# Attention and a gated feed-forward block: pair 0's transposes, the order of copies and loads on GpSimd, and the last output half

## The chip, the cores and the metric

The kernel runs on one core of a Trainium2 chip. The core has a matrix engine (TensorE, "PE" in the profile, whose weight loads are listed as "PEld"), VectorE ("DVE"), ScalarE ("ACT"), GpSimd ("POOL") and SyncE ("SP"). Each engine runs its own list of instructions in order and waits on semaphores that other engines and DMAs count up. DMAs are issued by SP, ACT and POOL and moved by 16 shared DMA engines. The metric is the device time of one execution in microseconds (us).

## The reference

The first part is softmax attention over 8 batches, 12 heads, 448 positions and 64 columns a head; the second is a feed-forward block on the 3584 x 768 result with weights of 768 x 1536 (gate and value) and 1536 x 768 (output). All inputs and the output are fp32.

```python
scores = scale * np.matmul(q, k.transpose(0, 1, 3, 2))
attn = softmax(scores)                       # over the last axis
x = np.matmul(attn, v).transpose(0, 2, 1, 3).reshape(B * S, H * D)
g = x @ w_gate
out = (g * (1.0 / (1.0 + np.exp(-g))) * (x @ w_val)) @ w_out
```

## The kernel before

**Tiling.** Heads are worked in pairs, 48 of them. The 448 positions of a head are 4 chunks of 112. For a pair, `qk_half` computes scores for two of the four chunks at a time, transposed (keys on the partitions): four matmuls of 448 columns into two double-bank PSUM tiles `s`, and one exponential on ScalarE for each tile (L194). `sums` adds up the exponentials with a matrix of ones, `recips` inverts the sums on VectorE, `pv` multiplies with V and `scaled` writes the normalized result into `X`, which is the transposed input of the feed-forward block. That block is cut into 8 pieces of 384 or 512 tokens. For each, `ffn1_steps` makes 12 gate and 12 value products with their activation, and `ffn2_steps` the output in chunks of 128 tokens, each in two halves of `OH` = 384 columns (12 accumulating matmuls per half, L252 or L255), copied from PSUM by ScalarE (L314) and stored.

**Operands of the scores.** Q and K must be turned so that the 64 head columns lie on the partitions. Three ways are used:
- Pair 0 is loaded as fp32 by SP, cast to fp16 by VectorE and ScalarE in `prep` (L153, L154; head 0 by the one, head 1 by the other), and turned by TensorE's transposes in `turn` (L170): eight for Q into one PSUM tile `tp`, a copy by VectorE (L172), a dummy matmul, eight for K into another tile, and a second copy (L176). Q lies in the upper half of `qkT` (columns from `NC` on), K in the lower.
- Pairs 1 to 10 are loaded as fp16 by POOL and turned by TensorE, 16 transposes and one copy each.
- Pairs from 11 (`NPE`) on are loaded by POOL, two pairs to a load (`load_qk16`: one DMA for Q, one for K, L118), copied by POOL into another order (`prep`, L156, two copies a pair), and turned by a DMA transpose issued by SP (L159).

**Order of the work.** It is written out by hand: every engine executes in the order in which the program issues. The loop over pairs `pr` issues for pair `pr` the first score half, the preparation of later pairs (`prep(pr + 3)` by POOL and SP, `prep(pr + 2)` where TensorE turns), pieces of the feed-forward block, and the second score half. At even `pr` from 8 on it first issues the load of pairs `pr + 6` and `pr + 7` on POOL's queue (L426 and L427), and then the two copies of `prep(pr + 3)` on the same queue (L438 and L439). V's loads (`load_v`, L127) and the weights' loads (L142, L144) use POOL's queue as well; the third part of `wo`, the output weights, is issued just ahead of the first of those even `pr`. A DMA of POOL waits for the landing of the DMA issued eight before it. `wo` is read for the first time by the output matmuls after piece 0 (L297 onwards), in thirds of four matmuls.

`dummy(n)` issues n matmuls of 512 columns on zeros. PSUM tiles come from three rings: `ps_s` (two tiles of two banks, for the scores), `ps_a` (one bank) and `ps_f` (three banks, for all else).

**The end.** The last 128 tokens' two halves have `osb` tiles of their own. The first half is copied by ScalarE and stored; the second half is one PSUM tile, copied as 192 columns by ScalarE (L309) and 192 by VectorE (L312), and then stored by two DMAs, 112 rows by SP and 16 rows by ACT (L324).

Of the kernel before, what the change touches and what calls it, by code (L numbers as in the profile page):

```python
# [10 lines left out]
FP32 = mybir.dt.float32  # L11
FP16 = mybir.dt.float16
AF = mybir.ActivationFunctionType
# [3 lines left out]
HS = 4096.0  # L17
# [3 lines left out]
LA = 6  # L21
# [6 lines left out]
def kernel(  # L28
# [23 lines left out]
    OH = DM // 2  # L52
# [41 lines left out]
    raw = {}  # L94
    v16 = {}
    qkT = {}
# [4 lines left out]
    def dummy(n):  # L101
        wp = ps_f.tile([128, 512], FP32, tag="f", name="wp")
        for _ in range(n):
            nc.tensor.matmul(wp[:], lhsT=warm[:, 0:128], rhs=warm[:], start=True, stop=True)
# [41 lines left out]
    def prep(pr):  # L146
        rq, rk = raw[pr]
        if pr == 0 or pr >= NPE:
            qk16 = attp.tile([P, 2, NC, 2, D], FP16, tag="qk16", bufs=3)
            for t, src in enumerate((rq, rk)):  # L150
                dst = qk16[:, 1 - t].rearrange("p c h d -> p h c d")
                if pr == 0:
                    nc.vector.tensor_copy(dst[:, 0], src[:, 0])  # L153
                    nc.scalar.activation(dst[:, 1], src[:, 1], AF.Copy)  # L154
                else:
                    nc.gpsimd.tensor_copy(dst, src)  # L156
        qkT[pr] = attp.tile([128, 2 * NC, P], FP16, tag="qkT", name="qkT", bufs=5)
        if pr >= NPE:
            nc.sync.dma_start_transpose(  # L159
                qkT[pr][:], qk16[:].rearrange("p t c h d -> p (t c h d)")  # L160
            )
            return None

        def turn():
            tp = ps_f.tile([128, 2 * NC, 128], FP16, tag="f", name="tp")
            for t in range(2):
                for c in range(NC):
                    for hx in range(2):
                        src = qk16[:, 1 - t, c, hx] if pr == 0 else raw[pr][t][:, hx, c, :]
                        nc.tensor.transpose(tp[ts(hx, 64), (1 - t) * NC + c, 0:P], src, ident[:])  # L170
                if pr == 0 and t == 0:
                    nc.vector.tensor_copy(qkT[pr][:, NC:], tp[:, NC:, 0:P])  # L172
                    dummy(1)
                    tp = ps_f.tile([128, 2 * NC, 128], FP16, tag="f", name="tp")
            hi = NC if pr == 0 else 2 * NC
            nc.vector.tensor_copy(qkT[pr][:, 0:hi], tp[:, 0:hi, 0:P])  # L176

        return turn

    def qk_half(pr, half, between=None):  # L180
        if half == 0:
# [68 lines left out]
    def mm(dst, lhsT, rhs, start, stop):  # L250
        if not tiled[0]:
            nc.tensor.matmul(dst, lhsT=lhsT, rhs=rhs, start=start, stop=stop)  # L252
            return
        for j in range(4):
            nc.tensor.matmul(  # L255
                dst[ts(j, 32), :], lhsT=lhsT[:, ts(j, 32)], rhs=rhs, start=start, stop=stop
            )
# [32 lines left out]

    def ffn2_steps(kk, c0, n, hts, last_block):
        for ch in range(n // 128):
            osb = fp.tile([128, DM], FP32, tag="osb", bufs=3)
            for oh in range(2):
                if last_block and ch == n // 128 - 1 and oh == 1:
                    osb = fp.tile([128, DM], FP32, tag="osb", bufs=3)
                op = ps_f.tile([128, 512], FP32, tag="f")  # L297
                for fb in range(NFB):
                    mm(
                        op[:, 0:OH],  # L300
                        lhsT=hts[:, fb, ts(ch, 128)],
                        rhs=wo[fb // (NFB // 3)][:, fb % (NFB // 3), ts(oh, OH)],
                        start=(fb == 0),
                        stop=(fb == NFB - 1),
                    )
                last = last_block and ch == n // 128 - 1
                if last and oh == 1:
                    m = OH // 2
                    nc.scalar.activation(  # L309
                        osb[:, OH : OH + m], op[:, 0:m], AF.Copy, scale=1.0 / HS  # L310
                    )
                    nc.vector.tensor_scalar_mul(osb[:, OH + m : DM], op[:, m:OH], 1.0 / HS)  # L312
                else:
                    nc.scalar.activation(osb[:, ts(oh, OH)], op[:, 0:OH], AF.Copy, scale=1.0 / HS)  # L314
                if oh == 1 or last:
                    m0, m1 = (oh * OH, oh * OH + OH) if last else (0, DM)
                    l0 = c0 + ch * 128
                    l = l0
                    while l < l0 + 128:
                        b, j = divmod(l, S)  # L320
                        c, p0 = divmod(j, P)
                        m = min(P - p0, l0 + 128 - l)
                        eng = nc.scalar if last and m < 64 else nc.sync
                        eng.dma_start(  # L324
                            out[ts(NB * kk + b, S), :].rearrange("(p c) m -> c p m", c=NC)[
                                c, p0 : p0 + m, m0:m1
                            ],
                            osb[l - l0 : l - l0 + m, m0:m1],
                        )
                        l += m  # L330
                yield NFB * OH / 2400.0
# [7 lines left out]
    with tc.manual_schedule():  # L339
# [82 lines left out]
        for pr in range(END):  # L422
            slots = 2 * (min([x for x in add_at if x > pr] + [END + 0.5]) - pr)
            odd = pr % 2 == 1
            turn2 = None
            if not odd and 14 <= pr + LA < NPAIR:  # L426
                load_qk16(pr + LA)  # L427
            if pr == FIRST:
                recip_act(pr - 2, sums(pr - 2))
                load_table("exp_and_others")  # L430
                halves = [pv(pr - 2, 0), pv(pr - 2, 1, ps_f)]
            if pr < NPAIR:
                qk_half(pr, 0, prep(2) if pr == 1 else None)
            if pr == 0:
                dummy(1)
                turn()
                dummy(1)
            if pr + 3 < NPAIR and pr + 3 >= NPE:  # L438
                prep(pr + 3)  # L439
            if pr + 2 < NPAIR:  # L440
                if 0 < pr < NPE - 2:
                    turn2 = prep(pr + 2)
                if (pr + 2) % GP == GP - 1 and 4 <= (pr + 2) // GP + 1 < NGRP:
                    load_v((pr + 2) // GP + 1)
            if pr == FIRST:
                for t in range(2):
                    scaled(pr - 2, t, halves[t])
                add_block(0)
                ffn_run(2.5)
            elif not odd and pr >= 2:  # L450
                deferred.extend(recips(pr - 2, sums(pr - 2)))
                if pr < FIRST:
                    pop_deferred(1)
            elif pr in (3, 5):
                halves.append(pv(pr - 3, 1, ps_f))
                pop_deferred(4)
                for t in range(2):
# [66 lines left out]
```

## Time and profile before

| | us |
|---|---|
| median of 4 runs (465.71 to 466.54) | 466.09 |
| the profiled execution | 466.54 |
| its span, first to last instruction | 464.7 |
| PE busy | 453.8 (98%) |
| ScalarE busy | 242.3 (52%) |
| VectorE busy | 237.1 (51%) |
| POOL busy | 102.4 (22%) |

Times in the profile are counted from the start of the span. "A <-B" behind an instruction tells how long its engine stood idle before it and what ended that. The rows of a time-ordered view have start, busy time, engine, line, operation, what it writes and reads, and how many instructions of the kind were merged into the row. "q" behind an engine's name is its sequencer: an instruction that issues a DMA or waits. The DMA view counts packets, megabytes and the time that packets took as a share of 16 engines; it can exceed 100%, since an engine has several packets under way. A matmul's recorded end is modelled: in a stream, matmuls follow each other at a shorter spacing than their recorded length.

### The profile page before, as it was taken

What the parts mean: (1) busy time and instruction counts of PE and PEld (TensorE: products, weight loads), DVE (VectorE), ACT (ScalarE), POOL (GpSimd) and SP (SyncE); (2) the same over time, 40 slices, a digit from 0 to 9 for tenths busy, and PEclk for the clock granted to TensorE, in tenths of its full rate; (3) what the DMA queues carried; (4) which work ended last, traced back from release to release, by engine and by line L of the source; (5) the groups of instructions that cost most, each with busy time, mean ns of one, the idle gap of its engine ahead of it and who ended that gap; (6) DMA issues with size and microseconds to landing.
All of it is one profiled execution on the core that took longest, in us unless ns stands there. A gap on an engine that the chain in (4) does not pass through costs nothing.

```text
span 464.7 us, 14107 instructions
## 1 busy us (share of the span) xinstructions
PE 453.8 (98%) x6356; PEld 227.2 (49%) x6356; DVE 237.1 (51%) x372; ACT 242.3 (52%) x350; POOL 102.4 (22%) x162
## 2 busy tenths in 40 slices
PE   7799999999999999999999999999999999999996
PEld 2345444444455555444455555444445556554453
DVE  2565764466764553655545645645555546334310
ACT  6797656655565555545555564545455562221221
POOL 8553606431250042302223040310200000000000
PEclk9899999999999999999999999999999999999999
DMA  9999999991893383951949384903703111100123
GB/s 134 196 199 209 204 180 177 213 150 23 110 130 57 67 102 52 155 74 23 137 53 118 71 118 86 144 3 75 97 10 55 37 37 35 36 20 16 35 68 102
DMA packets 78780, 44.23 MB, mean 95 GB/s; under 512 B 36608, under 2 KB 75264, under 8 KB 78720
## 3 DMA queue, kind: packets, MB, share of 16 engines
q0 software_dynamic: 39264, 23.37, 37.8%
q1 hardware_dynamic: 39392, 19.92, 23.8%
q8 instruction: 49, 0.80, 0.7%
q14 instruction: 11, 0.09, 0.1%
q10 hardware_dynamic: 64, 0.05, 0.0%
HBM read 47.19 MB, written 11.01 MB: 125 GB/s over the span
## 4 chain that ended last, share of the span: by engine, by line
PE 85%; DMA 12%; ACT 1%; POOL 1%; issue 0%; DVE 0%
PE gp L255 15%; PE op L252 14%; PE vp L255 12%; PE op L255 10%; PE vp L252 9%; PE s L187 8%; PE acc L203 7%; PE gp L252 7%; DMA wv<-in_moe_w_val_dram 6%; PE acc L225 4%; DMA qkT<-qk 3%; DMA wg<-in_moe_w_gate_dram 2%; ACT E L194 1%; DMA rq<-in_q_dram 1%; POOL k L118 0%
## 5 line engine op out<-in xcount | busy, mean ns | idle before, releaser
L194 ACT ACTIVATE E<-s 112x896 f16<-112x896 f32 x192 | 164.9, 916 | 28.7 <-PE s L187 28.7
L271 ACT ACTIVATE sg<-gp 128x384 f32<-128x384 f32 (+1 forms) x96 | 52.3, 545 | 85.4 <-PE gp L255 54.7
L283 DVE SCALAR_TENSOR_TENSOR t<-sg,gp 128x384 f32<-128x384 f32 (+1 forms) x96 | 58.6, 610 | 64.3 <-ACT sg L271 64.2
L314 ACT ACTIVATE osb<-op 128x384 f32<-128x384 f32 x55 | 27.0, 491 | 99.5 <-PE op L252 55.2
L255 PE MATMUL gp<-X,wg 128*32 128x512 f16 (+1 forms) x1416 | 78.1, 355 | 0.0
L240 DVE RECIPROCAL R<-ssb 128x112 f32<-128x112 f32 x92 | 73.1, 827 | 0.7
L286 DVE SCALAR_TENSOR_TENSOR hts<-t,vp 128x384 f16<-128x384 f32 (+1 forms) x96 | 59.6, 621 | 22.9 <-PE vp L255 7.9
L252 PE MATMUL op<-wo,hts 128*128 128x384 f16 x396 | 68.5, 326 | 0.0
L255 PE MATMUL vp<-X,wv 128*32 128x512 f16 (+1 forms) x1224 | 66.9, 353 | 0.0
L217 DVE TENSOR_TENSOR X<-acc,R 128x448 f16<-128x448 f32 x48 | 29.7, 624 | 66.1 <-PE acc L203 64.2
L252 PE MATMUL vp<-X,wv 128*128 128x384 f16 (+1 forms) x270 | 58.4, 352 | 0.0
L187 PE MATMUL s<-qkT 64*128 64x448 f16 x384 | 54.6, 356 | 2.8 <-ACT E L194 1.9
L255 PEld LDWEIGHTS <-wg 128*32 128x32 f16 x1416 | 37.8, 97 | 29.6
L252 PEld LDWEIGHTS <-hts 128*128 128x128 f16 x396 | 38.1, 98 | 28.8 <-issue 3.0
L255 PE MATMUL op<-wo,hts 128*32 128x384 f16 x1104 | 48.9, 326 | 0.0
L252 PE MATMUL gp<-X,wg 128*128 128x384 f16 (+1 forms) x222 | 47.4, 350 | 0.0
L127 POOL DMA_DIRECT2D vt<-in_v_dram x17 | 13.0, 764 | 149.5 <-PE acc L203 148.6
L203 PE MATMUL acc<-E,vt 112*32 112x448 f16 x768 | 45.2, 355 | 0.0
L255 PEld LDWEIGHTS <-wv 128*32 128x32 f16 x1224 | 32.7, 97 | 25.5
L252 PEld LDWEIGHTS <-wv 128*128 128x128 f16 x270 | 25.3, 98 | 26.9 <-issue 4.8
L255 PEld LDWEIGHTS <-hts 128*32 128x32 f16 x1104 | 29.5, 97 | 16.4
L237 DVE COPY ssb<-acc 128x448 f32<-128x448 f32 x23 | 14.4, 625 | 42.4 <-PE acc L225 42.4
(39 smaller groups left out, 208.3 us busy)
## 6 DMA issues: line engine op xcount, KB each, us to landing
vt<-in_v_dram POOLq DMA_DIRECT2D x15, 336.0 KB, 6.2
q<-in_q_dram POOLq DMA_DIRECT2D x22, 224.0 KB, 6.6
k<-in_k_dram POOLq DMA_DIRECT2D x22, 224.0 KB, 7.3
out_dram<-osb SPq DMA_DIRECT2D x7, 336.0 KB, 3.1
wo<-in_moe_w_out_dram POOLq DMA_DIRECT2D x3, 768.0 KB, 20.9
out_dram<-osb SPq DMA_DIRECT2D x8, 288.0 KB, 2.9
out_dram<-osb SPq DMA_DIRECT2D x8, 240.0 KB, 3.0
out_dram<-osb SPq DMA_DIRECT2D x8, 192.0 KB, 2.7
```

Of the source, the lines that this page charges most:

```text
L187: nc.tensor.matmul(s[:, hx, 0:S], lhsT=t[ts(hx, 64)].rearrange("p c q -> p (c q)")[:, c * P : c * P + 128], rhs=t[ts(hx, 64), NC:, :].rear ...
L194: nc.scalar.activation(E[pr][:, c], s[0:P, :, 0:S], AF.Exp, scale=sm_scale)
L203: nc.tensor.matmul(acc[ts(j, 32), 0:S], lhsT=v16[g][:, 2 * r + j % 2, c, :].rearrange("p (d t) -> p t d", t=2)[:, t], rhs=E[p0 + j // 2][: ...
L217: nc.vector.tensor_tensor(X[kk][:, hp + t, ts(bb, S)], acc[:, 0:S], R[p0][:], ALU.mult)
L225: nc.tensor.matmul(acc[ts(j, 32), 0:S], lhsT=ones[:], rhs=E[p0 + j // 2][:, c, j % 2, :], start=(c == 0), stop=(c == NC - 1),)
L240: lambda i=i: nc.vector.reciprocal(rt[:, ts(i, P)], ssb[:, ts(i, P)]) for i in range(4)
L252: nc.tensor.matmul(dst, lhsT=lhsT, rhs=rhs, start=start, stop=stop)
L255: nc.tensor.matmul(dst[ts(j, 32), :], lhsT=lhsT[:, ts(j, 32)], rhs=rhs, start=start, stop=stop)
L271: nc.scalar.activation(sg[:, 0:n], gp[:, 0:n], AF.Tanh, scale=0.5)
L283: nc.vector.scalar_tensor_tensor(t1[:, 0:n], sg[:, 0:n], 1.0, gp[:, 0:n], ALU.add, ALU.mult)
L286: nc.vector.scalar_tensor_tensor(hts[:, fb, 0:n], t1[:, 0:n], 0.5 * HS, vp[:, 0:n], ALU.mult, ALU.mult)
L314: nc.scalar.activation(osb[:, ts(oh, OH)], op[:, 0:OH], AF.Copy, scale=1.0 / HS)
```

## The change

Three places are changed.

- Pair 0 is turned by `turn0`: for Q and then for K, eight plain matmuls against the identity matrix write fp32 into a double-bank tile from the ring of the scores, chunks 0 and 1 in one bank and 2 and 3 in the other. VectorE copies the first bank and ScalarE the second. The dummy matmul between Q and K is gone.
- At even `pr`, the load of pairs `pr + 6` and `pr + 7` is issued behind `prep(pr + 3)` instead of ahead of the first score half, so that on POOL's queue the two copies come first.
- The last half of the output is two PSUM tiles of 192 columns. Each has 12 matmuls, a copy by ScalarE, and two stores (112 rows by SP, 16 rows by ACT).

```diff
+        def turn0():
+            for t in range(2):
+                tp = ps_s.tile([128, 2, 512], FP32, tag="s", name="tp")
+                for c in range(NC):
+                    for hx in range(2):
+                        nc.tensor.matmul(
+                            tp[ts(hx, 64), c // 2, ds(c % 2 * P, P)],
+                            lhsT=qk16[:, 1 - t, c, hx],
+                            rhs=ident[:],
+                            start=True,
+                            stop=True,
+                        )
+                dst = qkT[pr][:, ts(1 - t, NC)].rearrange("p (a c) q -> p a (c q)", a=2)
+                nc.vector.tensor_copy(dst[:, 0], tp[:, 0, 0 : 2 * P])
+                nc.scalar.activation(dst[:, 1], tp[:, 1, 0 : 2 * P], AF.Copy)
+
         def turn():
...
-                if pr == 0 and t == 0:
-                    nc.vector.tensor_copy(qkT[pr][:, NC:], tp[:, NC:, 0:P])
-                    dummy(1)
-                    tp = ps_f.tile([128, 2 * NC, 128], FP16, tag="f", name="tp")
-            hi = NC if pr == 0 else 2 * NC
-            nc.vector.tensor_copy(qkT[pr][:, 0:hi], tp[:, 0:hi, 0:P])
-
-        return turn
+            nc.vector.tensor_copy(qkT[pr][:], tp[:, :, 0:P])
+
+        return turn if pr else turn0
...
-                op = ps_f.tile([128, 512], FP32, tag="f")
-                for fb in range(NFB):
...
-                if last and oh == 1:
-                    m = OH // 2
-                    nc.scalar.activation(
-                        osb[:, OH : OH + m], op[:, 0:m], AF.Copy, scale=1.0 / HS
-                    )
-                    nc.vector.tensor_scalar_mul(osb[:, OH + m : DM], op[:, m:OH], 1.0 / HS)
-                else:
-                    nc.scalar.activation(osb[:, ts(oh, OH)], op[:, 0:OH], AF.Copy, scale=1.0 / HS)
...
+                parts = [(OH, OH // 2), (OH + OH // 2, OH // 2)] if last and oh else [(oh * OH, OH)]
+                for m0, w in parts:
+                    op = ps_f.tile([128, 512], FP32, tag="f")
+                    for fb in range(NFB):
...
+                    nc.scalar.activation(osb[:, ds(m0, w)], op[:, 0:w], AF.Copy, scale=1.0 / HS)
...
-            if not odd and 14 <= pr + LA < NPAIR:
-                load_qk16(pr + LA)
             if pr == FIRST:
...
             if pr + 3 < NPAIR and pr + 3 >= NPE:
                 prep(pr + 3)
+            if not odd and 14 <= pr + LA < NPAIR:
+                load_qk16(pr + LA)
```

More of the change, by code (lines that the diff above doesn't have):

```diff
@@ L168, in turn @@
                     for hx in range(2):
-                        src = qk16[:, 1 - t, c, hx] if pr == 0 else raw[pr][t][:, hx, c, :]
-                        nc.tensor.transpose(tp[ts(hx, 64), (1 - t) * NC + c, 0:P], src, ident[:])
-                if pr == 0 and t == 0:
-                    nc.vector.tensor_copy(qkT[pr][:, NC:], tp[:, NC:, 0:P])
-                    dummy(1)
-                    tp = ps_f.tile([128, 2 * NC, 128], FP16, tag="f", name="tp")
-            hi = NC if pr == 0 else 2 * NC
-            nc.vector.tensor_copy(qkT[pr][:, 0:hi], tp[:, 0:hi, 0:P])
-        return turn
+                        nc.tensor.transpose(
+                            tp[ts(hx, 64), (1 - t) * NC + c, 0:P], raw[pr][t][:, hx, c, :], ident[:]
+                        )
+            nc.vector.tensor_copy(qkT[pr][:], tp[:, :, 0:P])
+        return turn if pr else turn0
     def qk_half(pr, half, between=None):
@@ L292, in ffn2_steps @@
         for ch in range(n // 128):
-            osb = fp.tile([128, DM], FP32, tag="osb", bufs=3)
+            last = last_block and ch == n // 128 - 1
             for oh in range(2):
-                if last_block and ch == n // 128 - 1 and oh == 1:
+                if last or oh == 0:
                     osb = fp.tile([128, DM], FP32, tag="osb", bufs=3)
-                op = ps_f.tile([128, 512], FP32, tag="f")
-                for fb in range(NFB):
[L299 to L304, printed above, removed]
-                    )
-                last = last_block and ch == n // 128 - 1
-                if last and oh == 1:
-                    m = OH // 2
-                    nc.scalar.activation(
-                        osb[:, OH : OH + m], op[:, 0:m], AF.Copy, scale=1.0 / HS
-                    )
-                    nc.vector.tensor_scalar_mul(osb[:, OH + m : DM], op[:, m:OH], 1.0 / HS)
-                else:
-                    nc.scalar.activation(osb[:, ts(oh, OH)], op[:, 0:OH], AF.Copy, scale=1.0 / HS)
-                if oh == 1 or last:
-                    m0, m1 = (oh * OH, oh * OH + OH) if last else (0, DM)
+                parts = [(OH, OH // 2), (OH + OH // 2, OH // 2)] if last and oh else [(oh * OH, OH)]
+                for m0, w in parts:
+                    op = ps_f.tile([128, 512], FP32, tag="f")
+                    for fb in range(NFB):
+                        mm(
+                            op[:, 0:w],
+                            lhsT=hts[:, fb, ts(ch, 128)],
+                            rhs=wo[fb // (NFB // 3)][:, fb % (NFB // 3), ds(m0, w)],
+                            start=(fb == 0),
+                            stop=(fb == NFB - 1),
+                        )
+                    nc.scalar.activation(osb[:, ds(m0, w)], op[:, 0:w], AF.Copy, scale=1.0 / HS)
+                    if not last:
+                        m0, w = 0, DM
+                        if oh == 0:
+                            continue
                     l0 = c0 + ch * 128
@@ L325, in ffn2_steps @@
                             out[ts(NB * kk + b, S), :].rearrange("(p c) m -> c p m", c=NC)[
-                                c, p0 : p0 + m, m0:m1
+                                c, p0 : p0 + m, ds(m0, w)
                             ],
-                            osb[l - l0 : l - l0 + m, m0:m1],
+                            osb[l - l0 : l - l0 + m, ds(m0, w)],
                         )
```

## The prediction

> **What bounds the kernel now.** I read the engines' shares first, then what TensorE (PE) waited for, then the order in time around each of those waits, last the DMA records of the same stretch. The profiled execution took 466.54 us with a span of 464.7 us, so 1.84 us lie outside the span; it is the slowest of four runs, 0.45 us above their median of 466.09. I make the sum as a difference to the profiled execution and take it from the median.
>
> The page's shares, then PE's waits over the whole span (time, number, longest):
>
> ```profile
> PE 453.8 (98%) x6356; PEld 227.2 (49%) x6356; DVE 237.1 (51%) x372; ACT 242.3 (52%) x350; POOL 102.4 (22%) x162
> ```
> ```profile
> PE tp L170 <- DMA q<-in_q_dram: 1.0, 1, 1.0
> PE tp L170 <- DMA k<-in_k_dram: 0.9, 2, 0.7
> PE s L187 <- DMA qkT<-qk: 0.7, 1, 0.7
> ```
>
> PE is busy or queued without a gap from about 30 us to its last matmul, except for one wait of 0.71 us. So time can be won or lost only in three places: in the first 30 us, at that wait, and behind the last matmul. The wait and the first use of the output weights, PE's order in time from 64 us:
>
> ```profile
> 65.68 0.55 PE L187 MATMUL s<-qkT 64*128 64x448 f16 x4 [0.71 <-DMA qkT<-qk]
> ...
> 68.02 2.11 PE L252 MATMUL op<-wo,hts 128*128 128x384 f16 x12
> ```
>
> What is late there is the transpose of pair 11, the first one made by DMA. GpSimd (POOL) tells why:
>
> ```profile
> 44.19 0.74 POOL L144 DMA_DIRECT2D wo<-in_moe_w_out_dram  x1 [2.05 <-DMA wg<-in_moe_w_gate_dram]
> 46.97 0.71 POOL L118 DMA_DIRECT2D q<-in_q_dram  x1 [2.04 <-DMA wv<-in_moe_w_val_dram]
> 49.79 0.71 POOL L118 DMA_DIRECT2D k<-in_k_dram  x1 [2.11 <-DMA wv<-in_moe_w_val_dram]
> 50.50 0.62 POOL L156 COPY qk<-q 112x512 f16<-112x512 f16 x1
> 51.05 0.62 POOL L156 COPY qk<-k 112x512 f16<-112x512 f16 x1
> ```
>
> The two copies at L156 for pair 11 stand behind the load of pair 14, whose two DMAs each sat about 2 us until an older weight load had landed. SyncE (SP) issues the transpose at 51.70, and it lands 13.9 us later, at 65.63.
>
> The tail, in order of time:
>
> ```profile
> 457.98 2.28 PE L252 MATMUL op<-wo,hts 128*128 128x384 f16 x13
> ...
> 460.29 0.33 ACT L309 ACTIVATE osb<-op 128x192 f32<-128x192 f32 x1 [1.41 <-PE op L252]
> 460.65 0.36 DVE L312 TENSOR_SCALAR osb<-op 128x192 f32<-128x192 f32 x1 [17.10 <-ACT osb L309]
> 461.04 0.38 ACTq L324 DMA_DIRECT2D out_dram<-osb  x1
> ```
>
> VectorE (DVE) waits for ScalarE (ACT): the two halves of one bank are copied one after the other, and both last stores start at 461.04. The later one lands at 463.39; 1.3 us of closing semaphores follow.
>
> **The change part by part. GpSimd copies ahead of the load.** For pair 11 the two copies move ahead of the load of pair 14. In the built program they carry no wait of their own: an earlier load on the same queue has already waited for pair 10/11's data. They start when the third output-weight load has been issued, at 44.19 + 0.74 = 44.93, and end at about 46.1. The load behind them is held until 46.97 anyway, so it loses nothing. The transpose is issued at 46.1, 5.6 us earlier. With the same 13.9 us it lands at 60.0; PE asks for it at 65.68 - 0.71 = 64.97. The wait goes: -0.71 us there.
>
> What is late next decides how much of that stays. The DMA engines are full, and a transpose takes its turns from the loads. DMA records by queue (packets, MB, share), first in 54 to 55 us, then in 58 to 59 us with the transpose under way:
>
> ```profile
> q0 software_dynamic: 142, 0.21, 115.5%
> ```
> ```profile
> q0 software_dynamic: 113, 0.17, 93.9%
> q1 hardware_dynamic: 113, 0.03, 21.9%
> ```
>
> Packets alternate one for one, and the loads fall from 142 to 113 a microsecond. Per engine of 16 that is 113 ns for a load packet alone and 142 ns for the pair: about 27 ns for each transpose packet. A transpose has some 920 packets (about 58 an engine), so each one that is served ahead of a load sets it back 1.5 us. Before, pair 11's transpose and the start of pair 12's were served ahead of the end of the third output-weight load:
>
> ```profile
> DMA to landing us min/median/max: 23.0/23.0/23.0
> ```
>
> It was issued at 44.19 and landed at 67.23. PE reads that third at the ninth of the 12 matmuls starting at 68.02, which stand 0.1625 us apart: at 69.32, a slack of 2.1 us. In the changed kernel pair 11's transpose is through by 53 to 55 us. Pair 12's copies wait for their own data (landed 50.72 and 51.89), so its transpose is issued at about 52.8 instead of 53.12 and now has a free queue; with its first packets some 3 us after the issue, as I read them for pair 11, and 113 packets a microsecond it ends near 64.4. Pair 13's copies also move ahead of a load (55.19 to about 53.7), so a part of that transpose follows. Ahead of the load's end there is then about 1.1 transposes more than before: 1.1 x 1.5 = 1.6 us. It lands at about 68.9, plus up to 0.5 where packets run slow. PE, 0.71 earlier, asks at 68.61. I take 69.0: a new wait of 0.4 us, leaving -0.3 of the 0.71. Ends: -0.71 (landing by 68.6) and +0.5 (landing at 69.8).
>
> The other moves have cover. The second gate and value halves must land before the loads' order changes anything: value lands at 49.51, used at 50.08, and the transpose's packets start near 49.5 (issue 46.1 plus 3 to 3.7), so it is left alone; if not, its slack is 0.57. In all, 17 load pairs (34 DMAs) fall behind two copies each (1.2 us) and behind those copies' wait for a free buffer. The worst early case is the load of pair 20: 76.60 becomes 81.8 (pair 14's transpose lands at 80.57, then the copies). With its 11.7 to 12.6 us it lands by 95; its copies ran at 94.27, so they slip by 1 us, and the transpose behind them was issued only at 105.86. The V loads behind these on POOL slip as little. SP issues transposes earlier and stores no later. 0 us; without that cover, one more PE wait.
>
> **Pair 0.** Sixteen transposes become sixteen plain matmuls of the same 64x112 shape. The group took 0.44 us; I take the same. The dummy between them goes. Each fp16 copy of 448 columns (0.38 and 0.39 us, VectorE) becomes two fp32 copies of 224. VectorE's fp32 copies took 0.36 for 192 columns and 0.625 for 448, which gives 0.39 for 224; ScalarE's took 0.33 for 192 and 0.49 for 384, which gives 0.36. They don't run side by side: in the built program ScalarE's copy waits for VectorE's copy of the same tile. Around the start of pair 0's scores:
>
> ```profile
> 5.36 0.39 DVE L176 COPY qkT<-tp 128x448 f16<-128x448 f16 x1 [0.30 <-PE tp L170]
> 5.80 0.55 PE L187 MATMUL s<-qkT 64*128 64x448 f16 x4 [0.16 <-DVE qkT L176]
> 6.21 0.92 ACT L194 ACTIVATE E<-s 112x896 f16<-112x896 f32 x1 [1.33 <-PE s L187]
> ```
>
> The first two score matmuls need VectorE's part alone of K and both parts of Q: VectorE ends at 5.75, they start at 5.80 as before, and the first exponential at 6.21 is behind ScalarE's copy (5.79 to 6.15). The second pair of score matmuls waits until 6.2 instead of 6.0, and its exponential is due only at 7.02. So 0. Later waits for DMA cover it: PE waited 0.68 us for pair 2's K at 10.18 and for pair 3's at 12.69, set by loads alone. Ends: -0.1 and +0.3.
>
> **Last output half.** Twelve matmuls of 384 columns (0.1625 us apart) become 24 of 192. At half the spacing the last starts 0.08 later and drains 0.08 sooner: the end stays near 460.25, 0.03 later. The first part's ScalarE copy and its stores (issued at 459.7) lie beside the second part's matmuls. After the last matmul there is one ScalarE copy of 0.33 and no VectorE copy: stores at 460.68 instead of 461.04, -0.36. They are half as long; stores of 24 to 168 KB took 2.2 to 2.35 us to land here, so -0.06 more: -0.42. Ends: -0.65 (a 96 KB store took 1.8) and 0 (matmuls 98 ns apart, the length that the trace shows for a weight load: 24 x 98 = 2.35 us, +0.40).
>
> That length is more than the 81 ns of a half-size matmul; but pair 0's four score weight loads (64x128) stand within 0.11 us, so 98 ns is a latency, and I take 81. The Trainium skill's "TensorE: Matmul & The Clock Gate" (LDWEIGHTS) speaks against the change: it gives a weight load as columns / 1.2 ns, an estimate of 107 ns for 128 columns. If that couldn't be hidden, 24 x 107 would be 2.57 us against 1.95, and the part would cost 0.2 instead of winning 0.42. No row here has full-array loads this close together.
>
> Sum: -0.3 + 0 - 0.42 = -0.72; 466.09 - 0.72 = 465.4.
>
> **The rivals.** *The third output-weight load is on time* (B): all of 0.71 and the tail, -1.13, 464.9. For it: its 2.1 us of slack exceeds my 1.6 of lag, and PE needs only 68.6. Against it: the 0.3 us between is less than what I know of packet rates. *A new wait outgrows the old one* (C), the side of slower: the stretch 64 to 67 us moved 140 GB/s instead of 205 while a transpose was being issued beside one under way, a loss of 0.95 us. If pair 12's and pair 13's issue now both do that while the output weights move, the load lands at 67.23 + 1.6 + 1.9 = 70.7; PE stands 2.1 us instead of 0.71: +1.4 - 0.42 = +1.0, 467.1. It decides from a landing at 69.74. *Nothing to see* (D): the load lands at 69.3, so the wait has only moved, and the 192-column matmuls are bound by weight loads: 466.1.
>
> **How the numbers follow.** A (my sum) 0.42, B 0.32, C 0.15, D 0.11. The bound for a change that a measurement of this kernel can tell is 0.2%, 0.93 us: faster is below 465.16, slower above 467.02. B and a sixth of A are faster, most of C is slower by it, the rest within. The range takes the ends together: -1.5 (0.71 + 0.65 + 0.1) gives 464.6, and +0.8 (0.5 + 0 + 0.3) gives 466.9, which cuts off most of C.
>
> **What would show it.** No wait on qkT at pair 11; the first copies at L156 near 45 us; the transpose issued near 46 and landed before 61; a wait at the first op group, on wo, of 0 to 0.7 us. In the tail ScalarE's last copy at 460.3 relative to the old clock, stores 0.03 us later, last matmuls 81 ns apart. First exponential at 6.2. Wrong would be a wo landing later than 1.9 us after the old one, matmuls at 100 ns, or a half clock (0.50 from 14.5 to 17.5 us) that now begins earlier without the dummy.

## The result, and the profile after

The changed kernel took 467.67 us (median of 40 runs, 464.88 to 470.77) against 465.65 us for the kernel before (61 runs, 464.59 to 467.30). The ratio is 1.0046, with a 95% interval of 1.0035 to 1.0057: slower by half a per cent, where I had forecast 465.4 us and a range up to 466.9.

The profiled execution took 466.12 us with a span of 464.3 us. That is 1.5 us under the kernel's own median, and the runs now spread over 5.9 us instead of 2.7. One profile is therefore not a picture of this kernel; three more executions of it were profiled, and they are used below.

The first page line of the changed kernel, and what PE waited for longest:

```profile
PE 454.0 (98%) x6367; PEld 228.2 (49%) x6367; DVE 236.7 (51%) x371; ACT 243.2 (52%) x353; POOL 102.0 (22%) x162
```
```profile
PE s L199 <- ACT E L206: 2.1, 4, 0.8
PE wp L104 <- DVE ones L350: 1.2, 1, 1.2
PE op L264 <- DMA wo<-in_moe_w_out_dram: 1.1, 1, 1.1
PE tp L185 <- DMA q<-in_q_dram: 1.1, 1, 1.1
```

The shares are as before. The wait for qkT has left the list, and a wait for the third output-weight load (wo) is on it. PE's order in time from pair 11's scores on shows the exchange:

```profile
64.91 0.55 PE L199 MATMUL s<-qkT 64*128 64x448 f16 x4
...
67.25 1.46 PE L264 MATMUL op<-wo,hts 128*128 128x384 f16 x8
69.78 0.81 PE L264 MATMUL op<-wo,hts 128*128 128x384 f16 x4 [1.06 <-DMA wo<-in_moe_w_out_dram]
70.52 0.55 PE L199 MATMUL s<-qkT 64*128 64x448 f16 x4
```

The scores begin at 64.91 with no wait, 0.77 earlier than before. The first output half begins at 67.25, also 0.77 earlier, but stops after eight of its twelve matmuls: the ninth needs the third wo load, and starts at 69.78. Before, the group ran through from 68.02, so its ninth started at 69.32. GpSimd's (POOL's) order in time tells what moved:

```profile
43.29 0.74 POOL L144 DMA_DIRECT2D wo<-in_moe_w_out_dram  x1 [2.05 <-DMA wg<-in_moe_w_gate_dram]
44.02 0.62 POOL L156 COPY qk<-q 112x512 f16<-112x512 f16 x1
44.57 0.62 POOL L156 COPY qk<-k 112x512 f16<-112x512 f16 x1
46.09 0.71 POOL L118 DMA_DIRECT2D q<-in_q_dram  x1 [0.89 <-DMA wv<-in_moe_w_val_dram]
48.89 0.71 POOL L118 DMA_DIRECT2D k<-in_k_dram  x1 [2.10 <-DMA wv<-in_moe_w_val_dram]
```

The copies now run at 44.0, ahead of the load, and pair 11's transpose is issued at 45.2 and lands at 56.9. Pair 12's copies follow at 51.69 and 53.54, each behind its own data, and its transpose is issued at 54.18. From the issue of the third wo load to its landing (it was 23.0 us before):

```profile
DMA to landing us min/median/max: 26.4/26.4/26.4
```

Pair 0, in order of time:

```profile
5.36 0.39 DVE L177 CAST qkT<-tp 128x224 f16<-128x224 f32 x1 [0.28 <-PE tp L169]
5.79 0.36 ACT L178 ACTIVATE qkT<-tp 128x224 f16<-128x224 f32 x1 [0.31 <-DVE qkT L177]
5.81 0.75 PE L199 MATMUL s<-qkT 64*128 64x448 f16 x4 [0.16 <-DVE qkT L177]
...
6.21 1.73 ACT L206 ACTIVATE E<-s 112x896 f16<-112x896 f32 x2
```

And the tail:

```profile
458.83 1.90 PE L264 MATMUL op<-wo,hts 128*128 128x192 f16 x21
...
460.76 0.33 ACT L320 ACTIVATE osb<-op 128x192 f32<-128x192 f32 x1 [0.56 <-PE op L264]
461.13 0.38 ACTq L332 DMA_DIRECT2D out_dram<-osb  x1
```

Both are what the prediction described: the first exponential still starts at 6.21, and behind the last matmul there is one copy of 0.33 us instead of two in a row.

**One number for the whole rest.** PE waits for nothing from that first output half to its end. So the time of an execution should be the start of the ninth matmul plus a constant. Over the eighteen profiled executions of this study it is:

```
kernel          ninth matmul   time     difference
old tail:
before              69.32     466.54     397.22
turn0_alone         67.06     464.26     397.20
order_later         69.37     466.56     397.19
order_wo_free       68.49     465.65     397.16
order_alone2        70.83     468.00     397.17
order_first         68.91     465.94     397.03
t12_late            68.81     465.84     397.03
order_fill          70.98     468.15     397.17
order_fill13        70.24     467.42     397.18
order_alone         70.04     468.84     398.80
order_two           70.12     468.78     398.66
new tail:
after               69.78     466.12     396.34
after_again         70.54     466.89     396.35
after_p1            68.91     465.25     396.34
after_p2            69.93     468.00     398.07
tail_alone          68.21     464.48     396.27
two_parts           67.34     463.69     396.35
two_parts_t12       69.36     465.69     396.33
```

(Where the group ran through, its ninth matmul is taken at eight spacings of 0.1625 us behind the group's start; in turn0_alone, whose group took 0.07 us longer than that, it is read from the trace.) Three things are in this table. The constant is 397.0 to 397.2 with the old tail and 396.3 with the new one, so the new tail is worth 0.8 to 0.9 us. All else that the change does shows in the ninth matmul's start. That start differs between executions of one kernel too: five of the profiles (before, after, after_again, order_wo_free, order_alone2) have a half clock from about 14 to 18 us, and in these the group of twelve starts at 67.0 to 68.0; where neither that nor a wait on qkT delays PE, it starts at 65.7 to 66.5. And three executions have 1.5 to 1.7 us more: order_alone, order_two and after_p2. That last part was not in my prediction at all.

### The profile page after: what moved, and what is told of

It is laid out like the page before. It is cut to its first block, busy times and chain, and to the rows that moved or that the text cites. A ratio compares the mean times of both kernels' runs of the same rounds, so it can differ in the third digit from the quotient of the medians.

```text
span 464.3 us, 14131 instructions
## 1 busy us (share of the span) xinstructions
PE 454.0 (98%) x6367; PEld 228.2 (49%) x6367; DVE 236.7 (51%) x371; ACT 243.2 (52%) x353; POOL 102.0 (22%) x162
## 4 chain that ended last, share of the span: by engine, by line
PE 84%; DMA 13%; POOL 2%; issue 1%; ACT 0%; POOLq 0%
PE gp L267 15%; PE op L264 14%; PE vp L267 13%; PE op L267 10%; PE vp L264 9%; PE s L199 8%; PE acc L215 7%; PE gp L264 7%; DMA wo<-in_moe_w_out_dram 6%; DMA wg<-in_moe_w_gate_dram 5%; PE acc L237 4%; DMA q<-in_q_dram 2%; POOL q L118 1%; POOL k L118 0%; POOL vt L127 0%
## 5 line engine op out<-in xcount | busy, mean ns | idle before, releaser
L206 ACT ACTIVATE E<-s 112x896 f16<-112x896 f32 x192 | 164.8, 916 | 26.9 <-PE s L199 26.7
L320 ACT ACTIVATE osb<-op 128x384 f32<-128x384 f32 (+1 forms) x57 | 27.7, 486 | 101.8 <-PE op L264 57.5
L264 PE MATMUL op<-wo,hts 128*128 128x384 f16 (+1 forms) x408 | 68.7, 321 | 1.1 <-DMA wo<-in_moe_w_out_dram 1.1
L215 PE MATMUL acc<-E,vt 112*32 112x448 f16 x768 | 45.2, 355 | 0.0
L156 POOL COPY qk<-q 112x512 f16<-112x512 f16 x37 | 22.9, 620 | 63.0 <-DMA qkT<-qk 46.9
```

The costliest lines, as they stand in the source:

```text
L206: nc.scalar.activation(E[pr][:, c], s[0:P, :, 0:S], AF.Exp, scale=sm_scale)
L215: nc.tensor.matmul(acc[ts(j, 32), 0:S], lhsT=v16[g][:, 2 * r + j % 2, c, :].rearrange("p (d t) -> p t d", t=2)[:, t], rhs=E[p0 + j // 2][: ...
L320: nc.scalar.activation(osb[:, ds(m0, w)], op[:, 0:w], AF.Copy, scale=1.0 / HS)
```

## The experiments

### Each part alone, and the changed kernel again

order_alone moves the load behind the copies, and nothing else:

```
-            if not odd and 14 <= pr + LA < NPAIR:
-                load_qk16(pr + LA)
...
                 prep(pr + 3)
+            if not odd and 14 <= pr + LA < NPAIR:
+                load_qk16(pr + LA)
```

> The kernel before with the moved load alone. Theory W (the third output-weight load, set back by a transpose, is what costs; how far differs from execution to execution): this kernel carries the whole loss and more, since it lacks the tail's gain: +2 to +3.5 us against before in the median, wide spread of some 5 us, and its profile has a PE wait on wo at the first op group of 1 us or more. Rival K (the dummy matmul taken out of pair 0 lets the clock gate close once more in the first 20 us): no loss here beyond the 0.45 us that the profile of the changed kernel shows at wo, so 0 to +0.6.

turn0_alone takes only `turn0` for pair 0 as the diff of the change has it, tail_alone only the two parts of the last output half:

```
+        return turn if pr else turn0
```

> The kernel before with the new turn of pair 0 alone. Theory W: 0 (-0.3 to +0.3), first exponential at 6.2 us, half clock from about 14.5 to 17.5 us only. Rival K: +1.7 us for each further window at half clock, in part of the executions, so +1 to +3 in the median.

```
+                parts = [(OH, OH // 2), (OH + OH // 2, OH // 2)] if last and oh else [(oh * OH, OH)]
```

> The kernel before with the last half in two banks alone. Both theories: -0.4 to -0.9 us; last matmuls 81 to 83 ns apart, last stores 0.33 us after the last matmul's end, landing in 1.8 to 2.0 us.

after_again is the changed kernel, unchanged:

> The changed kernel once more. Both theories: +1.5 to +2.5 us in the median, spread of 4 to 6 us. Theory W: the profile's wait on wo is 1 us or more and its time differs from the first profile's by as much as that wait does. Rival K: the times go with the number of windows at half clock in the first 20 us.

All four stood against the same runs of before (465.79 us):

```
order_alone   468.22   1.0048 [1.0030, 1.0065]
turn0_alone   465.42   0.9988 [0.9974, 1.0002]
tail_alone    465.05   0.9990 [0.9977, 1.0003]
after_again   467.14   1.0040 [1.0017, 1.0063]
```

The loss is in the order alone: +2.4 us. The other two parts each gain a little in the median, but both intervals reach past 1, so alone neither gain is shown. In order_alone the ninth output matmul stands longer still:

```profile
70.04 0.81 PE L252 MATMUL op<-wo,hts 128*128 128x384 f16 x4 [2.35 <-DMA wo<-in_moe_w_out_dram]
```

### Is it the wait on the third wo load?

In order_wo_free the first output half reads its last four weight blocks from the second third of the weights instead, so that one half of one output block is computed with wrong weights; every instruction stays, only the wait goes. It is order_alone with:

```
-                        rhs=wo[fb // (NFB // 3)][:, fb % (NFB // 3), ts(oh, OH)],
+                        rhs=wo[min(fb // (NFB // 3), 1 if kk + c0 + ch + oh == 0 else 2)][
+                            :, fb % (NFB // 3), ts(oh, OH)
+                        ],
```

> All 17 loads moved, but the very first output half (12 matmuls, 128 tokens x 384 columns) reads the second third of the output weights where it should read the third, so that part of the output is wrong and nothing of that half waits for the third load. The same matmuls in the same order. Theory W: the loss is gone and the wait on pair 11's transpose with it: -0.3 to -1.0 us against before, no half clock near 70 us. Rival L: +1.5 to +2.4, as with the wait.

It took 464.75 us against 465.83, 0.9980 [0.9967, 0.9993]: 1.1 us faster than before. The load still took 26.3 us and landed at 69.81, but PE did not wait for it:

```profile
67.19 2.11 PE L252 MATMUL op<-wo,hts 128*128 128x384 f16 x12
```

That settles the place: all of the loss goes through this one wait, and without it the order gains 0.3 to 1.5 us by the interval, in which the 0.71 us of the qkT wait lies.

### Which of the seventeen moved loads does it?

order_first moves only the load issued at pair 8 (pairs 14 and 15), order_later only the other sixteen:

```
-            if not odd and 14 <= pr + LA < NPAIR:
+            if not odd and 14 <= pr + LA < NPAIR and pr != 8:
                 load_qk16(pr + LA)
...
+            if not odd and 14 <= pr + LA < NPAIR and pr == 8:
+                load_qk16(pr + LA)
```

(order_later has `==` and `!=` exchanged.)

> The kernel before with one load moved behind its two copies, that of pairs 14 and 15. Theory W (pair 11's and 12's transposes get ahead of the third output-weight load, which is late for the first output matmuls; the gap then closes the clock gate in part of the executions): the whole loss of the moved loads, +2 to +2.8 us; wait on wo of 1 to 2.5 us, landing at 69.5 to 71. Rival L (each of the 17 moved loads costs a little, by later landings or by a busier queue): +0.1 to +0.5, and a wait on wo under 1.1.

> The other 16 loads moved, that of pairs 14 and 15 left ahead of the copies. Theory W: 0 (-0.3 to +0.3); transpose of pair 11 issued near 51 us, third output-weight load landing near 67, no wait on wo. Rival L: +1.5 to +2.4.

order_first took 466.72 us, 1.0022 [1.0004, 1.0040], with a wait of 1.3 us and a load of 25.8 us. order_later took 466.18 us, 1.0001 [0.9989, 1.0013]: the wo load at 23.8 us, and the old wait for the transpose still there. PE's order in time of order_later:

```profile
65.73 0.55 PE L187 MATMUL s<-qkT 64*128 64x448 f16 x4 [1.55 <-DMA qkT<-qk]
...
68.07 2.11 PE L252 MATMUL op<-wo,hts 128*128 128x384 f16 x12
```

So the later loads cost nothing that these runs can tell (the interval is -0.5 to +0.6 us), as I had argued. order_two moves the loads at pairs 8 and 10 (`pr <= 10` behind, `pr > 10` ahead):

> The two loads at pairs 8 and 10 moved (pairs 14/15 and 16/17), the other 15 ahead of the copies. The first alone gave +0.9, all 17 gave +2.4, the later 16 alone 0. If the second load matters together with the first, since pair 13's transpose is then issued beside pair 12's while the output weights move: +2 to +2.8, landing of the third load at 69.7 to 70.5. If not (spread of the executions, or later loads): +0.6 to +1.2, landing near 69.

It took 468.0 us, 1.0043 [1.0021, 1.0065], with a wait of 2.1 us: by the medians the two loads together are nearly the whole loss of order_alone, and the first alone 0.9 us of it. The intervals of the two runs (+0.2 to +1.9 us and +1.0 to +3.0) overlap, so how the loss divides between the two loads is not shown.

### Can the order be kept without the loss?

t12_late moves the load at pair 8 only, and makes pair 12's copies one step later, so that its transpose is issued at 59.0 and not at about 53:

```
-            if not odd and 14 <= pr + LA < NPAIR:
+            if not odd and 14 <= pr + LA < NPAIR and pr != 8:
...
-            if pr + 3 < NPAIR and pr + 3 >= NPE:
+            if pr + 3 < NPAIR and pr + 3 >= NPE and pr != 9:
+                if pr == 10:
+                    prep(12)
                 prep(pr + 3)
+            if not odd and 14 <= pr + LA < NPAIR and pr == 8:
+                load_qk16(pr + LA)
```

> Only the load of pairs 14 and 15 moved (as in the run that gave +0.9), and pair 12's copies put one step later, behind the load of pairs 16 and 17, so that pair 12's transpose is issued near 58 us instead of 53. Theory W by its inner step (it is pair 12's transpose, served ahead of the third output-weight load, that sets it back): the load lands at 67.5 to 68.5, no wait on wo above 0.3, and the loss turns to -0.3 to -0.7. If pair 11's early transpose itself is the harm: landing stays near 69 and the loss at +0.7 to +1.2.

It took 466.36 us, 1.0009 [0.9996, 1.0022], with a load of 25.2 us and a wait of 1.1: pair 12's transpose is not the whole reason for the late load. The landing stayed near 69 (68.77), as expected if pair 11's early transpose does the harm; the loss of 0.5 us lies between the two expectations. Pair 12's transpose still moves beside the end of this load, from 62 us on, so pair 11's share is not isolated.

two_parts is the changed kernel with the load back in its old place, and two_parts_t12 is two_parts with t12_late's order:

> The changed kernel with the loads back ahead of the copies: pair 0's turn and the last half alone. Both theories: the two gains add, -0.7 to -1.3 us against before, with the tail 0.85 us shorter from the last matmul's end.

> The same order together with the new turn of pair 0 and the new last half. Theory W: below the two parts alone (464.94), at 464.2 to 464.8, -1.0 to -1.6 against before. If the order's loss stays: 465.5 to 466.

two_parts took 464.94 us against 465.83, 0.9980 [0.9965, 0.9995]: the best version apart from order_wo_free, 0.9 us faster than before. Its wo load took 23.5 us and its group ran through:

```profile
66.04 2.11 PE L264 MATMUL op<-wo,hts 128*128 128x384 f16 x12
```

two_parts_t12 took 466.80 us, 1.0026 [1.0004, 1.0049], where I had hoped for less than two_parts; it is also above the 465.5 to 466 that I expected if the order's loss stays. Its profile holds a stretch of 6.8 us at half clock from 12.3 us on, while before's has one of 3.4 us there; whether that is typical of it, one profile cannot tell. With PE that late, the load's 25.4 us were no wait at all.

### The clock behind the gap

In order_alone the granted clock falls to one half shortly behind the gap: PE goes on at 70.04, and the half clock lasts from 70.95 to 74.36 us. The stage (busy time of PE, PEld, DVE, ACT and POOL, granted clock, DMA share, GB/s):

```profile
71.00:74.40 3.40, 3.40 (x25) 1.06 (x22) 0.62 (x1) 2.00 (x3) 1.60 (x3) 0.51 1.51 192
```

Was that the gap's doing? order_fill fills it with eight dummy matmuls, order_fill13 with thirteen, in order_alone's kernel:

```
                 for fb in range(NFB):
+                    if kk + c0 + ch + oh == 0 and fb == 8:
+                        dummy(8)
```

> All 17 loads moved, as in the kernel with the moved loads alone (468.22), and eight dummy matmuls of 512 columns (1.7 us) put in front of the ninth matmul of the first output half, where PE waits for the third output-weight load. They fill most of the wait and add no time where it is over 1.7 us. Theory G (the gap of 1 to 2.5 us near 68 us closes PE's clock gate for 3.4 us in part of the executions, at 1.7 us each): the median falls by 0.5 to 1.2 us, to about 467.3, and no half clock stands near 70 us in the profile. Without G (the loss is the lateness alone): the median stays within 0.3 of 468.2.

> The same with 13 dummy matmuls (2.8 us) in front of the ninth matmul of the first output half, so that PE has next to no gap there. Theory G (the closing gate is about half of the loss): median 0.5 to 1.2 us below its partner's, all executions under 469.5, no half clock near 70 us. Without G: the same median as its partner or up to 0.4 above it, where the dummies outlast the wait.

order_alone2 is order_alone once more, on the same chip as order_fill13; after_p1 and after_p2 are two more profiled executions of the changed kernel:

> The kernel with all 17 loads moved, again, as the partner of the next. Both readings: +2 to +2.8 us, a wide spread up to 470; wait on wo of 1 to 2.5 us. Theory G: where the profile has a half-clock window near 70 us, the time from the ninth output matmul to pair 12's scores is 1.6 us longer than where it has none.

> The changed kernel, for one more profile. Both readings: third output-weight load landing 25.5 to 27 us after its issue, wait on wo of 1 to 2.5 us. Theory G: with a half-clock window behind that wait the time is above 468, without one below 467.5.

> As the one before: one more profile of the changed kernel, with the same numbers expected by both readings and by theory G.

```
order_fill    468.15 (467.06 to 468.66)  1.0048 [1.0033, 1.0063]  against 465.81
order_fill13  467.63 (467.40 to 468.93)  1.0044 [1.0028, 1.0060]  against 465.47
order_alone2  467.95 (465.11 to 470.95)  1.0047 [1.0025, 1.0069]  against 465.47
```

With eight dummies PE still waited 1.4 us for a load that landed at 70.94, and the clock stayed whole near 70 us; the median of 468.15 is what I had expected if the gap does not halve the clock. Thirteen dummies outlast the wait and leave no gap: in the profile they end 1.5 us after the load has landed (68.77), so they add time of their own. The median hardly moved (0.3 us lower than order_alone2, where I had expected 0.5 to 1.2), so as tests by the median both fills are misses. The spread is 1.5 us instead of 5.8: the slow end is gone, and so is the fast one, because the dummies always run.

The runs that were only timed say more, since each has its mean granted clock on record. In the eighteen profiled executions that mean is 0.996 or less in the nine with a half clock somewhere in the work, and 0.997 or more in the other nine. By this mark 18 of 23 runs of order_alone and order_alone2 had a half clock, and 5 of 18 runs of order_wo_free and order_fill13, which have the same order without the gap. The changed kernel had one in 32 of its 40 runs, before in 49 of the 105 runs that stood beside the experiments. Without one, the changed kernel took 466.3 us in the mean (8 runs) and before 465.7 (56 runs). So of the loss of 2.0 us some 0.6 are left where the clock stays whole; most of it is found where the clock fell. The mean clock does not tell where in the span it fell, and a half clock at 14 to 18 us counts as well.

The two profiled executions of the changed kernel show the place. PE's order in time and the stage behind the gap, first after_p1:

```profile
68.91 0.81 PE L264 MATMUL op<-wo,hts 128*128 128x384 f16 x4 [1.50 <-DMA wo<-in_moe_w_out_dram]
...
71.00 2.12 PE L264 MATMUL op<-wo,hts 128*128 128x384 f16 x12
73.06 0.55 PE L199 MATMUL s<-qkT 64*128 64x448 f16 x4
```
```profile
71.00:74.40 3.40, 3.40 (x36) 1.54 (x32) 0.62 (x1) 2.10 (x5) 2.45 (x5) 1.00 1.45 196
```

then after_p2:

```profile
69.93 0.81 PE L264 MATMUL op<-wo,hts 128*128 128x384 f16 x4 [2.80 <-DMA wo<-in_moe_w_out_dram]
...
72.90 2.84 PE L264 MATMUL op<-wo,hts 128*128 128x384 f16 x12
75.67 0.55 PE L199 MATMUL s<-qkT 64*128 64x448 f16 x4
```
```profile
71.00:74.40 3.40, 3.40 (x25) 1.19 (x22) 0.62 (x1) 1.89 (x3) 1.59 (x3) 0.50 1.49 193
```

From the ninth matmul to pair 12's scores it is 4.15 us in after_p1 and 5.74 in after_p2, with the clock at 1.00 in the one and 0.50 in the other: 1.59 us, the same excess as in the table above. The times are 465.25 and 468.00, where I had expected under 467.5 without the half clock and above 468 with it. The half clock followed gaps of 2.35, 2.15 and 2.80 us. It did not follow gaps of 1.06 to 1.50 us, nor two of 2.03 and 2.33 (after_again, order_alone2). So a gap of over 2 us here closes the gate (halves the granted clock) in part of the executions, and a shorter one was not seen to. The Trainium skill's "TensorE: Matmul & The Clock Gate" (What's actually happening) gives about 3.4 us of idle before the clock halves; the half-clock stretch of 3.4 us agrees with the window it names, but the gaps that closed the gate here were shorter.

## Why the prediction was wrong

**The failed step: the landing of the third wo load.** I let it land 1.6 us later against the old clock, plus up to 0.5, at 69.0, for a wait of 0.4; my bound for the wait's cost was +0.5, from a landing at 69.8. Counted from the issue at 44.19, that is a load of 24.8 us, at most 25.6. With the first load moved, issue to landing took 25.2 to 27.0 us in thirteen profiles, against 23.0 to 23.8 in the five with it ahead. That is 2.7 us more in the mean, and in the changed kernel's four profiles (25.9 to 26.7) PE stood 1.1 to 2.8 us instead of 0.4.

The step has two terms, and one held. The count of transposes served ahead of the load was right: by the DMA records there are 1430 to 1500 packets of the transposes' queue between the load's issue and its landing in the five profiles with the old order, and 2370 to 2460 in the eleven with the new one, so about one transpose or 1.5 us more, where I had 1.1 and 1.6. (In the two with pair 12's copies put later there are 1740 to 1750.) DMA records by queue of 44 to 66 us (packets, MB, share of 16 engines), before:

```profile
q0 software_dynamic: 3947, 4.00, 109.6%
q1 hardware_dynamic: 1282, 0.32, 12.6%
```

and after:

```profile
q0 software_dynamic: 3529, 3.63, 104.1%
q1 hardware_dynamic: 1836, 0.46, 22.5%
```

What I mis-sized is "plus up to 0.5 where packets run slow". In the stages around the now early transposes the engines are just as busy, but move far less. Stages of before:

```profile
50.00:52.00 2.00, 2.00 (x14) 1.10 (x12) 1.90 (x5) 0.72 (x2) 2.00 (x4) 1.00 1.39 199
52.00:54.00 2.00, 2.00 (x26) 0.77 (x25) 1.19 (x3) 1.77 (x3) 1.75 (x4) 1.00 1.20 212
54.00:56.00 2.00, 2.00 (x14) 0.88 (x12) 1.25 (x3) 0.69 (x2) 2.00 (x4) 1.00 1.15 208
```

and of after:

```profile
50.00:52.00 2.00, 2.00 (x14) 1.10 (x12) 1.90 (x5) 0.72 (x2) 0.31 (x1) 1.00 1.54 99
52.00:54.00 2.00, 2.00 (x26) 0.77 (x25) 1.19 (x3) 1.76 (x3) 0.77 (x2) 1.00 1.33 190
54.00:56.00 2.00, 2.00 (x14) 0.89 (x12) 1.25 (x3) 0.69 (x2) 1.55 (x4) 1.00 1.53 162
66.00:68.00 2.00, 2.00 (x19) 1.09 (x12) 1.71 (x4) 1.12 (x2) 0.00 (x0) 1.00 1.42 138
```

The last numbers are GB/s: 99 for 199, 162 for 208. A part of the fall is the transposes' small packets, which the first term counts. An estimate of the whole, from the rates of each microsecond between the load's issue and 2.3 us before its landing, with what is short of 203 GB/s counted as lost: 0.3 to 1.0 us in the five profiles with the old order, 1.4 to 2.6 us in the thirteen others, 1.4 more in the mean. Together with the 1.5 us of the first term that is close to the 2.8 us by which the load is later in the eleven. Before, the one stretch of this kind lay at 64 to 67 us, where the wo load was nearly through. I had seen that stretch, and used its 0.95 us for rival C only, twice, with 0.15 as its chance. The landing that C named, 70.7 or 26.5 us from the issue, is what came, and its time of 467.1 is near the 467.67. But that is in part luck: C wanted a transpose issued beside one under way, while at 50 to 52 us, the slowest stretch, none was being issued (45.23 and 54.18 are the nearest), and C knew nothing of the clock below. The lesson of the step is in the choosing: a slowdown that the trace of before shows once for one transpose belongs into the sum for every transpose that moves into the critical load's way, not into a rival.

The slack was a second size in this step that one profile hid. Of the 2.1 us, 0.71 were the wait on qkT itself, so 1.4 were left without that wait. The same difference in the other profiles with the old order is 0.9 us (tail_alone), 0.6 (order_later), 0.35 (two_parts) and nothing (turn0_alone, whose ninth matmul starts 0.04 us behind the landing); the last two had no wait on qkT to gain from. My sum was made from the execution with the most room.

**The missing step: the gap's clock.** I priced a gap on PE by its length. Where it was over 2 us, in some executions the clock halved for 3.4 us behind it, for 1.6 us more. I had named the half clock only for the dummy that left pair 0; by the median nothing came of it (turn0_alone 0.9988), though one profile without that dummy, two_parts_t12's, has the half clock earlier, from 12.3 us on. The longer wait and this step together make the loss: the ninth matmul at 70.04 with the half clock (order_alone) and at 70.83 without (order_alone2) stand for 468.8 and 468.0 us, where before's 69.32 stands for 466.5.

**What held.** The qkT wait went: copies at 44.0 (I had 45), transpose issued at 45.2 (46), landed at 56.9 (60). Only pair 12's transpose came later than I said, issued at 54.18 instead of 52.8. The sixteen later loads cost nothing that shows (order_later 1.0001). Pair 0 is neutral within its interval, and ScalarE's copy did wait for VectorE's copy of the same tile: 5.36 to 5.75, then 5.79, with the exponential at 6.21. The last 21 matmuls of 192 columns are 82.5 ns apart (from 458.83, 0.0825 each), against my 81. The 107 ns for 128 columns, an estimate from the formula in the Trainium skill's "TensorE: Matmul & The Clock Gate" (LDWEIGHTS), would have cost 0.2 us there if nothing hid it. That did not show: the trace lists these weight loads with 98 ns each, and the matmuls stand closer than that.

**The tail was better than I said.** From the last matmul's end to the end of the execution it was 4.49 us before and is 3.61 now, -0.88 against my -0.42 and outside my end of -0.65. From the last copies' start to the stores' issue it was 461.04 - 460.29 = 0.75 us and is 461.13 - 460.76 = 0.37, 0.38 less where I had worked out 0.36; the smaller stores landed in 1.76 to 1.93 us instead of 2.18 to 2.35, 0.42 less where I had allowed 0.06; under 0.1 is left over. So the size that was off is the landing of a half-size store. tail_alone has 0.74 of it in the median, with an interval that includes no gain, and that doesn't outweigh the wo load.

**What stays open.** Why the DMA engines run slow in those stretches. They lie where a transpose is issued or under way beside loads, but in other microseconds with one under way the engines moved their 200 (58 to 59 us of before), and t12_late, which pulls the transposes apart, kept a load of 25.2 us; no run here isolates one transpose beside one load.

Nor is it shown what decides whether a gap of 2.0 to 2.8 us closes the gate. One reading fits all ten profiles with a gap on wo, but no run tests it: that the clock is decided in steps of 3.41 us (the length of each half clock) which follow each other without a break. In the three executions with a half clock behind the gap, the 3.41 us ahead of its start (70.95, 71.62 and 70.97) hold 2.35, 1.9 and 2.4 us of the gap. In after_again and order_alone2, steps counted on from the early half clock's end (18.02 and 18.14) have a boundary near 69.2 and 69.3, inside the gap, so that no step holds more than about 1.5 us of it; and the five other gaps were 1.50 us or less.

## What to carry to other kernels

Before pulling a transfer forward, find the transfer that it will now share the DMA engines with, and its slack: here 0.71 us of waiting was removed in front of a load that had 2.1 us to spare in one execution and next to nothing in others, and the load lost 2.7 in the mean. Read a slack from several executions before a sum rests on it. Take the worst stretch that the old trace shows as a term of the sum for each transfer that moves, not as a rival. And price a stall of TensorE of more than about 2 us at its length plus a chance of a clock drop behind it (1.6 us here); when parts of a change are independent, as these three were, measure each alone and keep the ones that gain (two_parts, 0.9980 [0.9965, 0.9995]).

## What the runs showed of the hardware that I had not expected

- A PE gap of 2.15, 2.35 or 2.80 us between dense matmuls was followed by 3.4 us at a granted clock of 0.50, costing 1.5 to 1.7 us; after gaps of 2.03 and 2.33 us in other executions nothing followed.
- With a DMA transpose under way beside loads, the DMA engines moved 99 GB/s over two microseconds (50 to 52) in which before, with no transpose packet yet, had 199, at a higher busy share (1.54 against 1.39). With one under way at 58 to 59 us, before moved 201.
- Full-array weight loads that the trace lists with 98 ns each did not bound matmuls of 192 columns: 82.5 ns apart.
- Halving the last stores shortened issue to landing by about 0.4 us (2.18 to 2.35, then 1.76 to 1.93).
